# First visit's scores as plain float32 products of two heads on 64 rows each; the value products of a visit as one row

## The chip, the cores and the metric

The kernel runs on one core of one Trainium2 chip. The metric is the device time of one execution in microseconds; the time of a kernel is the median of several runs. A profile comes from one further execution with the hardware profiler on.

The core has five engines that matter here, each working through its own list of instructions in order: TensorE (PE, with its weight loads PEld), VectorE (DVE), ScalarE (ACT), GpSimd (POOL) and SyncE (SP), which issues the DMA transfers.

## The reference, cut to what matters

```
B, H, S, D = 4, 8, 768, 64
q_bucket = bits of (q @ proj > 0), 6 of them, as one number;  k_bucket likewise
scores = q @ k.T / 8, and -1e9 where q_bucket != k_bucket
attn = softmax(scores);  y = attn @ v              # for each batch and head
x = y as [B*S, 512]
out = (relu(x @ w_in) ** 2) @ w_out                # w_in 512 x 2048, w_out 2048 x 512
```

The feed-forward part is called `moe` in the code. The inputs q, k and v are float32; the weights come as 64-bit numbers, of which the kernel makes two float16 parts.

## The kernel before, in words

**Two layers of program.** The body of the kernel does not issue instructions. Each call, as `pe.matmul(...)` or `dve.tensor_scalar(...)`, appends an operation (`Op`) to a `Program`, with its possible engines, its dependencies and a rank. `Program.add` finds the dependencies by comparing the regions that operations touch (`Program.region`); a tile in PSUM counts as one region. `Program.order` then plans: it runs a list scheduler forwards with costs written down in the code (`Program.cost`), computes priorities backwards from the result, and repeats that four times (`ROUNDS`), keeping the shortest plan. `Program.emit` issues everything in that fixed order. So each change of the operations gives a new order of the whole kernel. A call of `matmuls` with several products is one operation, and nothing is placed inside it. Where the planner sees TensorE idle early in the program, `emit` fills part of the gap with products of ones (tile `idle`).

**Units, visits and stages.** A unit is 128 queries of one head against all 768 keys. A visit is a pair of heads and a half of the queries (384): six units. There are 192 units in 32 visits. Batch 0 takes the first halves of its four pairs of heads (visits 0 to 3) and then the second halves (visits 4 to 7); the later batches take both halves of a pair in turn. When the four visits of a batch and a half are there, a stage of the feed-forward part can run on these 384 rows: 16 steps over the hidden dimension, each of 12 products into `pm` (384 columns) and 9 into `po` (512 columns). There are eight stages. `PACE` keeps a product of the stages from running ahead of a given unit. Counted as `pace()` counts, a stage has 112 steps of three products each.

**Preparing a pair of heads** (`prep`). Keys and queries of a head arrive in one tile R, keys on partitions 0 to 63 and queries on 64 to 127. A is their float16 part, L the float16 rest. The signs of the projections (`pd`, `bits`) times a table of signs (`sgn`) give mask codes `pc`, which become M. Five copies by DMA between partitions then build, for each head, stacks of 128 rows: (Q, A) and (M, L). The scores of a unit are four float16 products (two stacks by two halves of the keys) accumulated in `pS`: main parts, cross terms and mask in 128 rows. The A, L, Q and M of four pairs are kept (8 buffers each), so that batch 0 prepares each pair once for both its halves.

**A unit** (`unit`). VectorE takes the scores from PSUM to `e` with the row's extreme, ScalarE takes the exponential with the row's sum, `rv` is its reciprocal. In the first four visits (`PLAIN_AV`) GpSimd multiplies `e` by `rv`, TensorE transposes it into `pT`, and ScalarE or VectorE copies it to `aT` as float32. Later visits make two float16 parts (`hl`) and transpose them by DMA into `aT`. `pS` has one buffer of two banks; until unit 24 every other unit uses the banks of `po`.

**The value products of a visit** (`av`). For both heads, on columns 0 to 63 and 64 to 127 of TensorE, `aT` is multiplied with the values into one bank, `pA`: 6 pairs of float32 products in the first four visits, 18 pairs of float16 products (hi by hi, lo by hi, hi by lo) after them. Each pair is one operation of the planner. The result, as two float16 parts, is `xx`.

**The start.** On SyncE's queue stand the first pair's R, two loads of `proj` to `pj`, eight of the sign table to `sgn_f`, then stacks, weights (`raw`) and further pairs as the planner orders them. Every operation is issued by lines 422 and 425, so the profile's groups are told apart by their tiles.

Of the kernel before, what the change touches and what calls it, by code (L numbers as in the profile page):

```python
# [11 lines left out]
F16 = mybir.dt.float16  # L12
BF16 = mybir.dt.bfloat16
F32 = mybir.dt.float32
# [3 lines left out]
AF = mybir.ActivationFunctionType  # L18
ALU = mybir.AluOpType
# [4 lines left out]
P = 128  # L24
B, H, S, D = 4, 8, 768, 64
NB = 6
HS = 384
UNITS = B * H * S // P
KC = S // P
# [3 lines left out]
BIG = float(2.0**100)  # L33
# [14 lines left out]
PREP, STACKS, VALUES = -9, 0, 2  # L48
# [3 lines left out]
ALTERNATE = {True: 24, False: 0}  # L52

PLAIN_AV, DIVIDE = (0, 1, 2, 3), ("pool",)
# [6 lines left out]
PACE = ((19, 0), (64, 140), (193, 660))  # L61

TOP_BY, LOW_BY = ("dve", "act"), ("dve", "pool")
CHECK_RANK, EARLY = 200, 24


# [61 lines left out]
class Program:  # L128
# [24 lines left out]
    @staticmethod  # L153
    def region(view):
        ap, rec = view.ap, view.rec
        size = lambda dims: 1 + sum(st * (n - 1) for st, n in dims)
        if rec.kind == "dram":
            return 0, 1, ap.offset, ap.offset + size(ap.ap), 0, 0, 0
        p0, f0 = divmod(ap.offset, rec.row)
        if rec.kind == "psum":  # L160
            return 0, 1, 0, 1, 0, 0, 0

        (step, n), inner = ap.ap[1], size(ap.ap[2:])
        block = (step, f0 % step, f0 % step + inner) if n > 1 and f0 % step + inner <= step else (0, 0, 0)
        return (p0, p0 + ap.ap[0][1], f0, f0 + size(ap.ap[1:])) + block
# [281 lines left out]
def run(ctx: ExitStack, tc, kq, v, proj2, w_in, w_out, consts, out, flag):  # L447
    fast = flag is not None
# [5 lines left out]
    pr = Program(tc)  # L454
    pe, dve, act, pool, sp = pr.pe, pr.dve, pr.act, pr.pool, pr.sp
    T, U = slice(0, D), slice(D, P)
# [3 lines left out]
    def send(out, x):  # L460
        sp.dma_start(out, x)
# [15 lines left out]
    def sb(shape, dtype, name, bufs=1, tag=None):  # L477
        return pr.tile(sbp, "sb", shape, dtype, name, bufs_of.get(tag or name, bufs), tag)

    def ps(shape, dtype, name, bufs=1, tag=None):  # L480
        return pr.tile(psp, "psum", shape, dtype, name, bufs, tag)
# [8 lines left out]
        sp.dma_start(cst, consts[:, 0:4])  # L490
    pj = sb([P, 32], F32, "pj")
    dve.memset(pj, 0.0)
    sp.dma_start(pj[:, 0:NB], proj2[:, NB : 2 * NB])
    sp.dma_start(pj[:, NB : 2 * NB], proj2[:, 3 * NB : 4 * NB])
    sgn_f = sb([P, 4 * P], F32, "sgn_f", tag="f" if fast else "o")
    dve.memset(sgn_f, 0.0)
    for n in range(4):
        for t in range(2):
            c0 = 4 + t * D
            sp.dma_start(sgn_f[32 * n + t * NB : 32 * n + (t + 1) * NB, n * P + t * D : n * P + (t + 1) * D], consts[2 * t * NB : (2 * t + 1) * NB, c0 : c0 + D])  # L500
    sgn = sb([P, 4 * P], BF16, "sgn")
    masks = cst
    if fast:
        parts = lambda x: x.rearrange("p (n t d) -> p n t d", t=2, d=D)
        dve.tensor_scalar(parts(sgn)[:, :, 0], parts(sgn_f)[:, :, 0], 2.0 / BIG, 2.0**15, ALU.mult, ALU.mult)
        dve.tensor_scalar(parts(sgn)[:, :, 1], parts(sgn_f)[:, :, 1], 2.0, 2.0**14, ALU.mult, ALU.mult)
        masks = sb([P, 2], F32, "masks")
        dve.memset(masks[T, 0:1], 3 * 2.0**16)
        dve.memset(masks[T, 1:2], -65504.0)
        dve.memset(masks[U, 0:1], 2.0**16)  # L510
        dve.memset(masks[U, 1:2], 0.0)
        balance = 1.0
        maxes, sums = sb([P, UNITS], F32, "maxes"), sb([P, UNITS], F32, "sums")
    else:
        dve.tensor_copy(sgn, sgn_f)
        balance = cst[:, 2:3]
    thr = sb([P, 1], F32, "thr")
    dve.memset(thr, -(2.0**-80))
    unit_f = sb([P, P], F32, "unit_f")
    sp.dma_start(unit_f, consts[:, 4 + 2 * P :])  # L520
    if not fast:
        ident = sb([P, P], BF16, "ident")
        dve.tensor_copy(ident, unit_f)
    ones = sb([P, P], BF16, "ones")
    dve.memset(ones, 1.0)
    pr.idle = ps([P, 512], F32, "idle", tag="pm")[:, 0:P], ones

# [89 lines left out]
    def matmuls(*args, start=True, stop=True):  # L619
        pr.add((pe, "matmuls", [(a, {"start": start, "stop": stop}) for a in args], {}))  # L620

    def prep(b, hp):
# [29 lines left out]
            out.append(((Q, A), (M, L)))  # L652
        return out

    vscales, loaded = {}, {}

    def scale_values(b):
# [36 lines left out]
        return VV  # L694


    def unit(st, half, i, aT, plain):
        c0 = half * HS + i * P
        u = pr.rank
        pS = ps([P, 3, 512], F32, "pS2", tag="po") if u % 2 and u < ALTERNATE[fast] else ps([P, 2, 512], F32, "pS")  # L700
        pr.marks[u] = len(pr.ops)
        pr.rank = u - 1000
        for s, (a, bb) in enumerate(st):
            for j in range(2):
                pe.matmul(pS[:, j, 0:HS], a[:, c0 : c0 + P], bb[:, j * HS : (j + 1) * HS], start=s == 0, stop=s == len(st) - 1)
        sS = pS[:, 0:2, 0:HS]
        e = sb([P, S], F32, "e", bufs_of["e"])
        e2 = e.rearrange("p (j s) -> p j s", j=2)
        if fast:
            nmx, sm = maxes[:, u : u + 1], sums[:, u : u + 1]  # L710
            dve.tensor_scalar(e2, sS, -SC, 2.0**40, ALU.mult, ALU.min, accum_out=nmx)
            act.activation(e2, e2, AF.Exp, bias=nmx, scale=-1.0, accum_out=sm)
        else:
            nmx, sm = sb([P, 1], F32, "nmx", 2), sb([P, 1], F32, "sm", 2)
            dve.tensor_reduce(nmx, sS, AX.XY, ALU.max, negate=True)
            act.activation(e2, sS, AF.Exp, bias=nmx, accum_out=sm)
        pr.rank = u
        rv = sb([P, 1], F32, "rv", 3)
        pr.add(*[(q, "tensor_scalar", (rv, sm, 1e-9, 1.0 if plain else 1.0 / ASC, ALU.add, ALU.mult), {}) for q in (dve, pool)])
        dve.reciprocal(rv, rv)  # L720
        if plain:
            move(e, e, rv, tuple(getattr(pr, k) for k in DIVIDE))
            for g in range(2):
                pT = ps([P, 512], F32, "pT", tag=("pm", "pA")[g] if u < EARLY else "misc")[:, 0:HS]
                pr.busy_from = min(pr.busy_from, len(pr.ops))
                for c in range(3):
                    kc = 3 * g + c
                    pe.matmul(pT[:, c * P : (c + 1) * P], e[:, kc * P : (kc + 1) * P], unit_f, start=True, stop=True, is_transpose=True)
                move(aT[:, 3 * g : 3 * g + 3, i * P : (i + 1) * P], pT.rearrange("p (c s) -> p c s", c=3), 1.0, (act, dve))
            return  # L730
        hl = sb([P, 2, S], F16, "hl", bufs_of["hl"])
        move(hl[:, 0], e, rv)
        left(hl[:, 1], e, rv, hl[:, 0])
        sp.dma_start_transpose(aT[:, :, i * P : (i + 1) * P], hl.rearrange("p t s -> p (t s)"))
# [5 lines left out]
    def av(b, hp, half, VV, aTs):  # L740
        pA = ps([P, 512], F32, "pA")[:, 0:HS]
        plain = VV.dtype == F32
        todo = [(kc, t * D, kc + l * KC) for t, l in (((0, 0),) if plain else ((0, 0), (1, 0), (0, 1))) for kc in range(KC)]
        scale = vscales[b][0] if plain else 1.0 / ASC
        for n, (kc, d0, c) in enumerate(todo):
            matmuls(*[(pA[m], VV[:, h, kc, d0 : d0 + D], aTs[h][:, c]) for h, m in enumerate((T, U))], start=n == 0, stop=n == len(todo) - 1)
        xx = xxs[b, half, hp] = sb([P, 2, HS], F16, "xx")
        move(xx[:, 0], pA, scale)
        left(xx[:, 1], pA, scale, xx[:, 0])
# [151 lines left out]
    kept, kept_v = {}, {}  # L901
    alive = lambda views: all(x.rec in x.rec.line[-x.rec.bufs :] for x in views)

    def ready(b, hp, rank):

        if (b, hp) not in kept or not alive(x for st in kept[b, hp] for ab in st for x in ab):
            pr.rank = rank
            kept[b, hp] = prep(b, hp)

    ready(*visits[0][:2], -10.0)  # L910

    early = {n: (split_win, j, win_rank(4 * j)) for j, n in enumerate(WIN_AT)}
    early[WOUT_AT] = split_wout, 0, conv_rank(0)
    done, u, stages = {}, 0, 0
    for n, (b, hp, half) in enumerate(visits):
        sts, aTs, plain = kept[b, hp], [], fast and n in PLAIN_AV
        for h, st in enumerate(sts):
            aT = sb([P, KC, HS], F32, "aT") if plain else sb([P, 2 * KC, HS], F16, "aT")
            aTs.append(aT)
            for i in range(3):  # L920
                pr.rank = u
                unit(st, half, i, aT, plain)
                u += 1
        if n + 1 < len(visits):
            ready(*visits[n + 1][:2], u + PREP)
        if (b, hp, plain) not in kept_v or not alive([kept_v[b, hp, plain]]):
            pr.rank = u - 6 + PREP
            kept_v[b, hp, plain] = values(b, hp, plain)
        pr.rank = u - 0.5
        av(b, hp, half, kept_v[b, hp, plain], aTs)  # L930
        if n in early:
            do, j, pr.rank = early[n]
            do(j)
        done[b, half] = done.get((b, half), 0) + 1
        if done[b, half] == H // 2:
            moe(stages, b, half)
            stages += 1
# [37 lines left out]
```

## Time and profile before

| | |
|---|---|
| median of 3 runs | 852.07 us (851.78 to 855.12) |
| profiled execution, its own time | 855.38 us |
| its span | 853.6 us |
| PE busy | 816.5 us, 96% |
| ACT busy | 655.9 us, 77% |
| DVE busy | 607.8 us, 71% |
| DMA queue q1, share of 16 engines | 76.6% |
| mean granted clock of TensorE | 0.994 |

An engine's busy time is the union of its instructions' times. A group of instructions is written as engine, operation, output<-input by the names of the tiles, partitions x elements, and count; then the busy time in us and the mean duration in ns of one, and the idle time of the engine just before them with what ended it. TensorE's products are pipelined: a product shows about 0.17 us longer than the time after which the next one starts, so starts are compared, not durations. A float32 product is listed as two instructions.

### The profile page before, as it was taken

How to read it: one execution, taken by the hardware profiler on the slowest of the kernel's cores; microseconds unless marked ns; L12 is line 12 of the kernel's file. 1: busy time of each engine (PE TensorE's matmuls, PEld its weight loads, DVE VectorE, ACT ScalarE, POOL GpSimd, SP SyncE). 2: the span in 40 equal slices, each digit the busy share in tenths (PEclk: the TensorE clock that was granted, in tenths of full speed). 3: DMA queues.
4: the chain of work that ended last, by engine and by line, in shares of the span. 5: the costliest groups of instructions: out<-in, count | busy, mean ns of one | idle time of the engine just before them, and what ended most of it. 6: DMA issues, size and time to landing. Idle time of an engine off the chain costs nothing.

```text
span 853.6 us, 14638 instructions
## 1 busy us (share of the span) xinstructions
PE 816.5 (96%) x5154; PEld 431.1 (51%) x5154; DVE 607.8 (71%) x1218; ACT 655.9 (77%) x1237; POOL 74.7 (9%) x149
## 2 busy tenths in 40 slices
PE   6788799999999999999999999999999999999996
PEld 5544445555555555555555555555554445544553
DVE  5789889998989898998988328999994171163111
ACT  3689999998988898888888557898894298743343
POOL 0246311000001000010100000110000000000000
PEclk9999999999999999999999999999999999999999
DMA  7996689999999999999999229999850089881001
GB/s 211 256 290 192 203 220 191 196 195 190 190 201 178 176 215 179 213 192 194 182 203 220 53 74 193 203 183 185 150 107 1 16 212 282 267 292 61 1 1 41
DMA packets 299297, 145.30 MB, mean 170 GB/s; under 512 B 268880, under 2 KB 279248, under 8 KB 299216
## 3 DMA queue, kind: packets, MB, share of 16 engines
q1 hardware_dynamic: 299216, 144.30, 76.6%
q8 instruction: 42, 0.69, 0.3%
q14 instruction: 39, 0.32, 0.1%
HBM read 56.17 MB, written 6.29 MB: 73 GB/s over the span
## 4 chain that ended last, share of the span: by engine, by line
PE 83%; ACT 6%; DMA 6%; DVE 3%; issue 1%; SPq 0%; POOL 0%; ACTq 0%
PE po L425 28%; PE pm L425 27%; PE pS L425 13%; PE pA L422 11%; DMA raw<-w_out 1%; PE pd L422 1%; ACT e L425 1%; ACT top L425 1%; ACT aT L425 1%; DMA raw<-w_in 1%; DMA X<-vp 1%; DMA V<-vp 1%; PE pc L425 1%; DMA M<-Q 1%; DMA X<-kq 1%
## 5 line engine op out<-in xcount | busy, mean ns | idle before, releaser
L425 PE MATMUL po<-wo,g 128*128 128x512 f16 x1152 | 326.3, 380 | 4.3 <-DVE g L425 3.2
L425 PE MATMUL pm<-xx,win 128*128 128x384 f16 x1536 | 316.0, 326 | 0.9 <-DVE xx L425 0.7
L425 PEld LDWEIGHTS <-win 128*128 128x128 f16 x1536 | 149.5, 98 | 112.5 <-issue 5.2
L425 ACT ACTIVATE e<-e,maxes 128x768 f32<-128x768 f32 x192 | 178.7, 932 | 25.2 <-DVE e L425 22.3
L425 DVE TENSOR_SCALAR_CACHE_REDUCE e<-pS 128x768 f32<-128x768 f32 x192 | 182.7, 953 | 16.4 <-PE pS L425 12.3
L425 DVE SCALAR_TENSOR_TENSOR hl<-e,rv,hl 128x768 f16<-128x768 f32 x168 | 170.8, 1019 | 15.1 <-ACT hl L425 14.3
L425 PEld LDWEIGHTS <-g 128*128 128x128 f16 x1152 | 110.9, 98 | 128.4 <-issue 10.0
L425 DVE SCALAR_TENSOR_TENSOR g<-g,g 128x384 f16<-128x384 f32 x124 | 68.5, 553 | 136.0 <-ACT g L425 132.1
L425 ACT ACTIVATE hl<-e,rv 128x768 f16<-128x768 f32 x168 | 155.0, 924 | 8.3 <-DMA aT<-hl 6.3
L425 ACT ACTIVATE g<-pm 128x384 f32<-128x384 f32 x127 | 61.4, 483 | 110.6 <-PE pm L425 109.5
L425 ACT ACTIVATE g<-g 128x384 f16<-128x384 f32 (+1 forms) x249 | 128.6, 517 | 5.3 <-PE po L425 1.6
L422 PE MATMUL pA<-aT,VV 128*64 128x384 f16 x1008 | 100.0, 331 | 0.0
L425 PE MATMUL pS<-A,Q 128*128 128x384 f16 x384 | 96.4, 330 | 3.3 <-DVE e L425 1.9
L425 PE MATMUL pS<-L,M 128*128 128x384 f16 x384 | 96.1, 328 | 2.0 <-DMA M<-Q 2.0
L425 POOL TENSOR_SCALAR rv<-sums 128x1 f32<-128x1 f32 x113 | 39.1, 346 | 569.0 <-ACT e L425 454.2
L422 PEld LDWEIGHTS <-VV 128*64 128x64 f16 x1008 | 51.8, 109 | 47.3 <-issue 29.8
L425 PEld LDWEIGHTS <-Q 128*128 128x128 f16 x384 | 34.3, 98 | 42.8 <-issue 17.9
L425 PEld LDWEIGHTS <-M 128*128 128x128 f16 x384 | 37.0, 98 | 29.3 <-DMA M<-Q 3.8
L425 DVE TENSOR_SCALAR M<-pc,masks 128x384 f16<-128x384 f32 x64 | 43.0, 671 | 6.6 <-PE pc L425 6.5
L425 ACT ACTIVATION_READ_ACCUMULATOR e<-e,maxes 128x1 f32 x192 | 37.0, 193 | 0.0
L425 DVE SCALAR_TENSOR_TENSOR L<-R,A 128x768 f16<-128x768 f32 x32 | 30.2, 950 | 6.3 <-ACT A L425 6.2
L425 ACT ACTIVATE A<-R 128x768 f16<-128x768 f32 x32 | 26.7, 836 | 8.3 <-DMA R<-kq 8.2
(68 smaller groups left out, 528.7 us busy)
## 6 DMA issues: line engine op xcount, KB each, us to landing
R<-kq SPq DMA_DIRECT2D x32, 384.0 KB
X<-kq SPq DMA_DIRECT2D x32, 384.0 KB
raw<-w_in SPq DMA_DIRECT2D x16, 511.8 KB
raw<-w_out SPq DMA_DIRECT2D x16, 511.8 KB
V<-vp SPq DMA_DIRECT2D x20, 384.0 KB
out<-o SPq DMA_DIRECT2D x24, 256.0 KB
X<-vp SPq DMA_DIRECT2D x16, 384.0 KB
Q<-L SPq DMA_DIRECT2D x32, 96.0 KB
```

Of the source, the lines that this page charges most:

```text
L422: ins = q.engine.matmul(*map(real, args), **kw).ins
L425: ins = getattr(q.engine, o.name)(*map(real, o.args), **{k: real(x) for k, x in o.kw.items()}).ins
```

## The change

It has three parts. The first visit (`WIDE` = 1) is not prepared by `prep`: a new function `first` loads keys K (64 rows of each of the two heads, one head on partitions 0 to 63, the other on 64 to 127) and queries G likewise, and makes mask codes MK and MG of 64 rows with one product for each half of the keys and one for the queries. `side_by_side` then computes the scores as a float32 product of G and K and a float16 product of MG and MK for each half of the keys, the two heads on rows 0 to 63 and 64 to 127; for the first two units the heads are taken one after the other, for the rest a product of each head forms one operation. The units of the two heads then alternate. The pair of heads of visit 0 is prepared by `prep` for visit 4. Second, `av` collects all products of a visit and adds them in operations of up to `2 * RUN` = 36. Third, `Program.region` tells banks of PSUM apart, and the constants come in fewer DMA transfers, with `ones` made earlier.

```
+RUN = 18
+CONSTS_BY, WIDE = ("sp", "sp", "sp"), 1
...
         if rec.kind == "psum":
-            return 0, 1, 0, 1, 0, 0, 0
+            return 0, 1, f0 // 512, 1 + (f0 % rec.row + size(ap.ap[1:]) - 1) // 512, 0, 0, 0
...
-    sp.dma_start(pj[:, 0:NB], proj2[:, NB : 2 * NB])
-    sp.dma_start(pj[:, NB : 2 * NB], proj2[:, 3 * NB : 4 * NB])
+    by[0].dma_start(pj[:, 0 : 3 * NB], proj2[:, NB : 4 * NB])
...
     for n in range(4):
-        for t in range(2):
-            c0 = 4 + t * D
-            sp.dma_start(sgn_f[32 * n + t * NB : 32 * n + (t + 1) * NB, n * P + t * D : n * P + (t + 1) * D], consts[2 * t * NB : (2 * t + 1) * NB, c0 : c0 + D])
+        by[1].dma_start(sgn_f[32 * n : 32 * n + 4 * NB, n * P : (n + 1) * P], consts[0 : 4 * NB, 4 : 4 + P])
...
+        codes = sb([P, 4 * P], BF16, "codes")
+        for t, x in enumerate((2.0 / BIG, 2.0)):
+            for j in range(2):
+                w = slice(2 * j, 2 * j + 2)
+                move(parts(codes)[:, w, t], parts(sgn_f)[:, w, t], x * 2.0 ** (15 - j), (dve,))
...
+    def first(hp):
+
+        K, G = [sb([P, n], F32, name, tag="VV") for name, n in (("K", S), ("G", HS))]
+        for x, w in ((K, T), (G, U)):
+            for odd, m in enumerate((T, U)):
+                send(x[m], kq[0, 2 * hp + odd, w, 0 : x.shape[1]])
+        MK, MG = sb([P, S], F16, "MK", tag="M"), sb([P, HS], F16, "MG", tag="Q")
+        halves = K[:, 0:HS], K[:, HS:], G
+        pd = ps([P, 512], F32, "pd", tag="misc")[:, 0:HS]
+        matmuls(*[(pd[32 * n : 32 * n + 32], pj, x) for n, x in enumerate(halves)])
+        bits = sb([P, HS], BF16, "bits")
+        act.activation(bits[0:96], pd[0:96], AF.Sign, scale=2.0**60, bias=thr[0:96])
+        pc = ps([P, 3, 512], F32, "pc", tag="po")[:, :, 0:HS]
+        for n in range(3):
+            pe.matmul(pc[:, n], codes[0:96, n * P : (n + 1) * P], bits[0:96], start=True, stop=True)
+        for n in range(2):
+            dve.tensor_scalar(MK[:, n * HS : (n + 1) * HS], pc[:, n], 3 * 2.0**16, -65504.0, ALU.subtract, ALU.max)
+        pr.add((act, "activation", (MG, pc[:, 2], AF.Relu), {"bias": shift}), (dve, "tensor_scalar", (MG, pc[:, 2], 2.0**16, 0.0, ALU.subtract, ALU.max), {}))
+        return K, G, MK, MG
+
+    def side_by_side(st, half, i):
+
+        K, G, MK, MG = st
+        c0 = half * HS + i * P
+        pr.rank = u - 1000
+        both = [ps([P, 2, 512], F32, "pS"), ps([P, 3, 512], F32, "pS2", tag="po")]
+        jobs = [[(n, x[:, j, 0:HS], a[m, c0 : c0 + P], bb[m, j * HS : (j + 1) * HS]) for x, m in zip(both, (T, U))] for n, (a, bb) in enumerate(((G, K), (MG, MK))) for j in range(2)]
+        if not i:
+            jobs = [[x[t]] for t in range(2) for x in jobs]
+        for x in jobs:
+            matmuls(*[y[1:] for y in x], start=x[0][0] == 0, stop=x[0][0] == 1)
+        return both
...
+        jobs = []
         for n, (kc, d0, c) in enumerate(todo):
-            matmuls(*[(pA[m], VV[:, h, kc, d0 : d0 + D], aTs[h][:, c]) for h, m in enumerate((T, U))], start=n == 0, stop=n == len(todo) - 1)
+            jobs += [((pA[m], VV[:, h, kc, d0 : d0 + D], aTs[h][:, c]), {"start": n == 0, "stop": n == len(todo) - 1}) for h, m in enumerate((T, U))]
+        for n in range(0, len(jobs), 2 * RUN):
+            pr.add((pe, "matmuls", jobs[n : n + 2 * RUN], {}))
...
+        if fast and visit < WIDE:
+            pr.rank = rank
+            wide[visit] = first(hp)
+        elif (b, hp) not in kept or not alive(x for st in kept[b, hp] for ab in st for x in ab):
             pr.rank = rank
             kept[b, hp] = prep(b, hp)
...
+        if n in wide:
             for i in range(3):
-                pr.rank = u
-                unit(st, half, i, aT, plain)
-                u += 1
+                for aT, pS in zip(aTs, side_by_side(wide[n], half, i)):
+                    pr.rank = u
+                    unit(None, half, i, aT, plain, pS)
+                    u += 1
```

More of the change, by code (lines that the diff above doesn't have):

```diff
@@ L492, in run @@
     dve.memset(pj, 0.0)
-    sp.dma_start(pj[:, 0:NB], proj2[:, NB : 2 * NB])
-    sp.dma_start(pj[:, NB : 2 * NB], proj2[:, 3 * NB : 4 * NB])
+    ones = sb([P, P], BF16, "ones")
+    dve.memset(ones, 1.0)
+    pr.idle = ps([P, 512], F32, "idle", tag="pm")[:, 0:P], ones
+    by = [getattr(pr, x) for x in CONSTS_BY]
+    by[0].dma_start(pj[:, 0 : 3 * NB], proj2[:, NB : 4 * NB])
     sgn_f = sb([P, 4 * P], F32, "sgn_f", tag="f" if fast else "o")
@@ L506, in run @@
         dve.tensor_scalar(parts(sgn)[:, :, 1], parts(sgn_f)[:, :, 1], 2.0, 2.0**14, ALU.mult, ALU.mult)
-        masks = sb([P, 2], F32, "masks")
+        masks = sb([P, 4], F32, "masks")
         dve.memset(masks[T, 0:1], 3 * 2.0**16)
@@ L511, in run @@
         dve.memset(masks[U, 1:2], 0.0)
+        codes = sb([P, 4 * P], BF16, "codes")
[3 more added lines that the diff above has]
+                move(parts(codes)[:, w, t], parts(sgn_f)[:, w, t], x * 2.0 ** (15 - j), (dve,))
+        shift, thr = masks[:, 2:3], masks[:, 3:4]
+        dve.memset(shift, -(2.0**16))
+        dve.memset(thr, -(2.0**-80))
         balance = 1.0
@@ L516, in run @@
         balance = cst[:, 2:3]
-    thr = sb([P, 1], F32, "thr")
-    dve.memset(thr, -(2.0**-80))
+    if not fast:
+        thr = sb([P, 1], F32, "thr")
+        dve.memset(thr, -(2.0**-80))
     unit_f = sb([P, P], F32, "unit_f")
-    sp.dma_start(unit_f, consts[:, 4 + 2 * P :])
+    by[2].dma_start(unit_f, consts[:, 4 + 2 * P :])
     if not fast:
@@ L523, in run @@
         dve.tensor_copy(ident, unit_f)
-    ones = sb([P, P], BF16, "ones")
-    dve.memset(ones, 1.0)
-    pr.idle = ps([P, 512], F32, "idle", tag="pm")[:, 0:P], ones
     win = sb([P, 2, NCC, DFF], F16, "win")
@@ L694, in values, with unit @@
         return VV
-    def unit(st, half, i, aT, plain):
+    def unit(st, half, i, aT, plain, pS=None):
         c0 = half * HS + i * P
         u = pr.rank
-        pS = ps([P, 3, 512], F32, "pS2", tag="po") if u % 2 and u < ALTERNATE[fast] else ps([P, 2, 512], F32, "pS")
         pr.marks[u] = len(pr.ops)
         pr.rank = u - 1000
-        for s, (a, bb) in enumerate(st):
-            for j in range(2):
-                pe.matmul(pS[:, j, 0:HS], a[:, c0 : c0 + P], bb[:, j * HS : (j + 1) * HS], start=s == 0, stop=s == len(st) - 1)
+        if pS is None:
+            pS = ps([P, 3, 512], F32, "pS2", tag="po") if u % 2 and u < ALTERNATE[fast] else ps([P, 2, 512], F32, "pS")
+            for s, (a, bb) in enumerate(st):
+                for j in range(2):
+                    pe.matmul(pS[:, j, 0:HS], a[:, c0 : c0 + P], bb[:, j * HS : (j + 1) * HS], start=s == 0, stop=s == len(st) - 1)
         sS = pS[:, 0:2, 0:HS]
@@ L902, in run, with ready @@
     alive = lambda views: all(x.rec in x.rec.line[-x.rec.bufs :] for x in views)
-    def ready(b, hp, rank):
-        if (b, hp) not in kept or not alive(x for st in kept[b, hp] for ab in st for x in ab):
+    wide = {}
+    def ready(visit, rank):
+        b, hp, _ = visits[visit]
+        if fast and visit < WIDE:
+            pr.rank = rank
+            wide[visit] = first(hp)
+        elif (b, hp) not in kept or not alive(x for st in kept[b, hp] for ab in st for x in ab):
             pr.rank = rank
             kept[b, hp] = prep(b, hp)
-    ready(*visits[0][:2], -10.0)
+    ready(0, -10.0)
     early = {n: (split_win, j, win_rank(4 * j)) for j, n in enumerate(WIN_AT)}
@@ L915, in run @@
     for n, (b, hp, half) in enumerate(visits):
[L916 to L919, printed above, removed]
+        plain = fast and n in PLAIN_AV
+        aTs = [sb([P, KC, HS], F32, "aT") if plain else sb([P, 2 * KC, HS], F16, "aT") for _ in range(2)]
+        if n in wide:
             for i in range(3):
-                pr.rank = u
-                unit(st, half, i, aT, plain)
-                u += 1
+                for aT, pS in zip(aTs, side_by_side(wide[n], half, i)):
+                    pr.rank = u
+                    unit(None, half, i, aT, plain, pS)
+                    u += 1
+        else:
+            for aT, st in zip(aTs, kept[b, hp]):
+                for i in range(3):
+                    pr.rank = u
+                    unit(st, half, i, aT, plain)
+                    u += 1
         if n + 1 < len(visits):
-            ready(*visits[n + 1][:2], u + PREP)
+            ready(n + 1, u + PREP)
         if (b, hp, plain) not in kept_v or not alive([kept_v[b, hp, plain]]):
```

## The prediction

> **What bounds the kernel now.** I read the page's first lines and its chain of waits first, then a table of windows cut where the character of the work changes, and last the order of time on single engines at the two places that the change touches.
>
> ```profile
> span 853.6 us, 14638 instructions
> PE 83%; ACT 6%; DMA 6%; DVE 3%; issue 1%; SPq 0%; POOL 0%; ACTq 0%
> ```
>
> The chain that ends last is TensorE for 83% of the span. Where the other 17% lie, the windows show (columns: stretch, length, busy time of PE, PEld, DVE, ACT, POOL, granted clock, DMA share, GB/s):
>
> ```profile
> 10.00:35.00 25.00, 17.64 (x195) 12.52 (x191) 16.75 (x26) 11.54 (x17) 0.00 (x0) 0.93 0.96 272
> 35.00:60.00 25.00, 20.51 (x130) 11.80 (x131) 20.66 (x46) 22.71 (x48) 14.33 (x19) 0.93 1.00 282
> 60.00:108.00 48.00, 39.13 (x246) 21.76 (x245) 43.11 (x91) 47.45 (x102) 22.37 (x31) 1.00 0.69 209
> 150.00:300.00 150.00, 149.97 (x991) 79.59 (x992) 136.53 (x290) 134.74 (x247) 9.62 (x27) 1.00 1.00 190
> 300.00:475.00 175.00, 175.00 (x1144) 91.84 (x1142) 155.71 (x322) 155.14 (x282) 12.48 (x34) 1.00 1.01 198
> 475.00:700.00 225.00, 224.85 (x1367) 115.88 (x1366) 152.03 (x291) 161.23 (x299) 9.82 (x26) 1.00 0.62 121
> 700.00:841.00 141.00, 137.32 (x755) 69.13 (x753) 39.02 (x68) 77.57 (x169) 0.00 (x0) 1.00 0.47 146
> ```
>
> From 150 us to 841 TensorE is never free for more than 4 us in all: there, time goes away only if TensorE work, or dead time inside its row, goes away. Before 108 us it is another program: ScalarE is busy 47.45 of 48 us from 60 on, VectorE 43.11, and between 10 and 35 us ScalarE stands idle for 25 - 11.54 = 13.5 us while DMA is at 0.96. The handover is the first product of the feed-forward layers (tile pm):
>
> ```profile
> 31.87 0.95 DVE L425 TENSOR_SCALAR_CACHE_REDUCE e<-pS 128x768 f32<-128x768 f32 x1
> 35.21 0.91 ACT L425 ACTIVATE e<-e,maxes 128x768 f32<-128x768 f32 x1
> ...
> 109.50 1.95 PE L425 MATMUL pm<-xx,win 128*128 128x384 f16 x11 [0.68 <-DVE xx L425]
> ```
>
> So the first unit's scores reach VectorE at 31.87 us, its exponential starts at 35.21, and layers of the first half can run from 109.5 on, released by the last xx of visit 3. Everything earlier than that is paid as TensorE's time without its filler.
>
> **The values' products in one row.** The row of one pair of value products among products of the layers, and the one visit that already runs in one piece, stand so in order of time:
>
> ```profile
> 774.60 0.35 PE L422 MATMUL pA<-aT,VV 128*64 128x384 f16 x2
> 774.89 0.39 PE L425 MATMUL po<-wo,g 128*128 128x512 f16 x1
> 775.21 0.35 PE L422 MATMUL pA<-aT,VV 128*64 128x384 f16 x2
> ...
> 506.19 3.12 PE L422 MATMUL pA<-aT,VV 128*64 128x384 f16 x36
> 509.24 2.12 PE L425 MATMUL po<-wo,g 128*128 128x512 f16 x9
> ```
>
> Nine po in a row last 2.12 us with the last one's 0.39, so one follows another after (2.12 - 0.39)/8 = 0.216 us. The 36 of a whole visit, 18 pairs that run two at a time, take 509.24 - 506.19 = 3.05 us with their exit, so a pair is at most 0.169 and, with an exit of some 0.12, 0.163 us. The alternating stretch repeats after 775.21 - 774.60 = 0.61 us: 0.61 - 0.163 - 0.216 = 0.23 us of each turn is neither product. It is the price of going from the 128*128 shape to 128*64 and back, and the rows call it busy. There are 95 such rows of f16 value products, the first and the last of them being
>
> ```profile
> 143.60 0.52 PE L422 MATMUL pA<-aT,VV 128*64 128x384 f16 x4
> 780.05 0.35 PE L422 MATMUL pA<-aT,VV 128*64 128x384 f16 x2
> ```
>
> for 28 visits. After the change each visit's 36 products are one operation of the planner (twice RUN), so 28 rows are left: 67 turns less, 67 x 0.23 = 15.4 us of TensorE's row. Their place decides what they are worth: 11 of the 67 lie before 300 us, 14 from 300 to 475, 42 after. After 475 nothing but TensorE is near its limit (VectorE 152 of 225 us, DMA 0.62), and those 42, 9.7 us, come off the end. Before 475 the units (scores, exponential, transposes) run beside DMA at 1.00 and VectorE at 0.91 of the time, and TensorE can only use what it saves if it has layers' products waiting. Up to 300 us it has done
>
> ```profile
> L425 PE MATMUL pm<-xx,win 128*128 128x384 f16 x352 | 66.2, 326 | 0.9 <-DVE xx L425 0.7 <-ACT g L425 0.2
> L425 PE MATMUL po<-wo,g 128*128 128x512 f16 x252 | 64.5, 380 | 0.7 <-ACT g L425 0.4 <-DVE g L425 0.2
> L425 PE MATMUL pS<-A,Q 128*128 128x384 f16 x178 | 45.3, 333 | 3.1 <-DVE e L425 1.7 <-DMA A<-A 1.3
> ```
>
> (352 + 252)/3 = 201 of the 224 steps that the first two of eight stages hold, at unit 178/2 = 89, and the third stage needs visit 14, which ends with unit 90 and some time for its transposes. 23 steps are 23 x 3 x (0.163 + 0.216)/2 = 13 us of stock, just enough. So the 11 x 0.23 = 2.5 us saved before 300 may only bring a wait forward: bounds 0 and 2.5, and I take half, as the units themselves are freed a little. This part gives 15.4 - 1.3 = 14.1 us, bounds 9.7 and 15.4.
>
> The edit has a cost: a score product that comes up during a visit's block waits up to 3.05 us, and behind it VectorE's e, ScalarE's exponential and the transposes of that unit. What hides it is that VectorE and ScalarE have other work (splits of earlier units, squares of the layers) and that no unit is on the chain after 475. If that cover is gone it costs what the stock of 13 us can't hold.
>
> The Trainium skill, TensorEngine Tiling (Array Packing), section Tiling Modes, says that a change of tiling mode drains TensorE; the 0.23 us agree, and by that rule the scores on 64 rows below pay it too, whose shape no row shows. At the 0.23 us of the rows, twelve operations of the first visit would pay 2.8 us, before 35 us, where it is covered as their own time is.
>
> **The first visit.** Removed from the start: two splits (A, L), ten copies that build the stacks, four mask products with their four M, and the wait for them. Added: K and G loaded to 64 rows for each of two heads, three mask products, float32 score products. Removed, the work comes back: the keys and queries of the same pair of heads are prepared for visit 4, between 60 and 108 us.
>
> When are the first scores there? Their inputs' chain is the one that can be read from the old start up to its first mask:
>
> ```profile
> 7.15 0.85 PE L422 MATMUL pd<-R,pj 128*32 128x384 f32 x8
> 9.77 0.68 DVE L425 TENSOR_SCALAR M<-pc,masks 128x384 f16<-128x384 f32 x1 [2.36 <-PE pc L425]
> ...
> 86.29 4.09 PE L422 MATMUL pA<-aT,V 128*64 128x384 f32 x24 [1.22 <-ACT aT L425]
> 90.31 0.34 PE L425 MATMUL pS<-A,Q 128*128 128x384 f16 x1
> ```
>
> The masks are ready at about 9.77 + 3 x 0.68 = 11.8 us, ahead of any stack. No row shows a float32 product on 64 rows. The nearest are the float32 value products, which run in pairs on 64 columns: (90.31 - 86.29)/6 = 0.67 us a pair. If rows pair as columns do, the visit costs 4 x 0.67 + 4 x 0.163 for its first two units, done singly, and as much for the other four: 6.7 us; if they don't pair, 10.0; the old 24 products cost 24 x 0.163 = 3.9. I take 6.7, the row of the same width. The difference, 2.8 to 6.1 us, lies between 10 and 35 us, where 25 - 17.64 = 7.4 us of TensorE are free, beside the products that the program puts in only to keep it busy. It costs the end nothing, at most it puts the sixth unit 6 us later, long before 35.
>
> The clock in those windows is 0.93, not 1.00. The Trainium skill, TensorE: Matmul & The Clock Gate, Part 1, says that the clock is either full or half and falls to half after an idle window of about 3.4 us. By that page alone a cold first visit would take 13.4 us in place of 6.7, and the units would still be through before 35.
>
> So six units start at about 13 us in place of 31.87. On ScalarE a unit is
>
> ```profile
> L425 ACT ACTIVATE e<-e,maxes 128x768 f32<-128x768 f32 x27 | 25.6, 953 | 0.0
> L425 ACT ACTIVATE aT<-pT 128x384 f32<-128x384 f32 x46 | 21.6, 505 | 2.8 <-PE pT L425 2.7
> L425 ACT ACTIVATE A<-R 128x768 f16<-128x768 f32 x9 | 7.7, 850 | 7.2 <-DMA R<-kq 7.0
> L425 DVE TENSOR_SCALAR_CACHE_REDUCE e<-pS 128x768 f32<-128x768 f32 x27 | 25.3, 951 | 1.6 <-PE pT L425 1.6
> L425 DVE TENSOR_SCALAR M<-pc,masks 128x384 f16<-128x384 f32 x17 | 11.4, 672 | 4.7 <-PE pc L425 4.7
> L425 DVE SCALAR_TENSOR_TENSOR L<-R,A 128x768 f16<-128x768 f32 x8 | 7.6, 956 | 4.3 <-ACT A L425 4.3
> ```
>
> 25.6/27 = 0.95 us of exponential and 2 x 21.6/46 = 0.94 of copies, 1.9 us, six times 11.3 us. All of it now lies after 35 us and would fit the 13.5 us that ScalarE idles before. Of the work that comes back, two A are 1.7 us: ScalarE's load from 35 to 108 falls from 70.2 to 60.6 of 73 us. VectorE is the next one late. It loses four of the six e (two were already before 35), 3.8 us, and gets two L and four M, 1.9 + 2.7 = 4.6, so its 20.66 + 43.11 = 63.8 stay 64.6 us. Were it never idle, the stretch would last 64.6 in place of 73, 8.4 us less; at the 96% that ScalarE holds there now (70.2 of 73) it lasts 67.3, 5.7 us less. DMA gets two R of 384 KB and ten stacks of 96 KB, 1.7 MB, at 209 GB/s 8 us; from 60 to 108 us it has 0.31 x 48 = 15 us free. I take 5.7, bounds 0 (visit 1's stacks come no sooner) and 8.4.
>
> The rest has one answer. Fewer, larger loads of constants, the ones and memsets moved ahead, codes from sgn_f (four small VectorE operations of some 0.3 us) lie before 10 us, under the loads. Regions of PSUM by bank free the planner's order among banks and remove no instruction. K and G sit in two of the five value buffers and are given back before the fourth value is needed.
>
> **Sum.** The profiled execution took 855.38 us, 1.8 more than its span, and 3.3 more than the median of 852.07. 855.38 - 14.1 - 5.7 = 835.6; the same 19.8 off the median are 832.3. With both at their bounds: 852.07 - 23.8 = 828.3 to 852.07 - 9.7 = 842.4.
>
> **Rivals.**
> - Only the value products pay. Visit 1 still waits for its stacks, which queue behind weights on a DMA at 1.00 from 35 to 60 us, so the engines are early with visit 0 and idle after it. For it: that share, and that the weights' conversions, which would fill the gap, wait for DMA too. Against it: ten stacks fewer are in that queue. 852.07 - 14.1 = 838.
> - Only the start pays. The units run at the pace of DMA and VectorE, TensorE's stock of layers' products runs dry, and what the rows save turns into waits, also late. For it: the stock of 13 us at 300. Against it: 42 of 67 turns lie after 475. 852.07 - 5.7 = 846.4.
> - Slower: a block stands in TensorE's row ahead of work that is ready, and waits at its head for the last transposed probabilities, because the fixed order was made with transposes that land sooner than they do with DMA at 1.00. The float32 block above already waited 1.22 us for its input. At this price in each of 28 visits it is 34 us, and 852.07 + 34 - 19.8 = 866; it outweighs the gains from 19.8/28 = 0.71 us a visit on. Against it: no f16 row of value products had any idle time ahead of it.
> - It doesn't do what it says in time: the whole order is planned anew, and a worse order later (an early pause of the units, a late weight) eats the 20 us. 852.
>
> **How the numbers follow.** The forecast has 0.60, the value products alone 0.20, the start alone 0.06, the wait at the block 0.06, no change 0.08. A measurement of this kernel can tell 0.5%, 4.3 us, from no change: faster is 0.60 + 0.20 + 0.06 = 0.86, same 0.08, slower 0.06. The predicted time is 832.3. The range goes from 824, 4 us under the bound for what a new order may add, to 847, which takes in the first two rivals; some 0.16 are left out.
>
> **What would show it.** Right: 28 rows of f16 value products of 36, each about 3.05 us to the next start, no idle time ahead of them; first e on VectorE at 12 to 14 us, the first pm at about 103 and TensorE full from there; VectorE at 95% or more before it. Wrong: the first pm at 109 as now with ScalarE idle between 30 and 45 us (the first rival); TensorE idle around 300 us with pm waiting for xx (the second); value products with a wait on DMA of the transposes ahead of them (the third). Float32 rows of the first visit whose starts are 0.67 us apart for each head, not for two, would show that rows don't pair.

## The result and the profile after

| | before | after |
|---|---|---|
| median of four runs each, in one comparison | 852.86 us | 833.34 us (830.51 to 834.86) |
| ratio, 95% interval | | 0.9764 (0.973 to 0.9798) |
| profiled execution | 855.38 us | 834.86 us |
| its span | 853.6 us | 833.1 us |

The forecast was 832.3 us. The page's head, after:

```profile
span 833.1 us, 14383 instructions
PE 794.3 (95%) x5001; PEld 430.0 (52%) x5001; DVE 605.2 (73%) x1200; ACT 656.6 (79%) x1238; POOL 72.7 (9%) x175
```

TensorE's busy time fell by 816.5 - 794.3 = 22.2 us, the others' hardly. To see where, I cut both traces at the handover, the first pm. First the windows of before, then those of after (columns as in the prediction):

```profile
0.00:108.50 108.50, 84.79 (x652) 52.59 (x653) 85.44 (x177) 85.75 (x170) 37.20 (x55) 0.97 0.80 231
108.50:853.60 745.10, 731.66 (x4504) 378.54 (x4502) 522.37 (x1042) 570.15 (x1068) 37.47 (x95) 1.00 0.77 161
```

```profile
0.00:97.70 97.70, 74.65 (x485) 43.33 (x485) 79.60 (x175) 80.62 (x162) 36.09 (x53) 0.97 0.83 242
97.70:833.10 735.40, 719.65 (x4517) 386.65 (x4516) 525.58 (x1026) 575.96 (x1077) 36.65 (x122) 1.00 0.77 166
```

The handover comes 108.5 - 97.7 = 10.8 us sooner, and what follows it is 745.1 - 735.4 = 9.7 us shorter. Behind the handover TensorE is busy 12.0 us less and idle 735.4 - 719.65 = 15.8 us, 2.3 more than the 13.4 before.

The order of time at the start, after: VectorE's first e, TensorE's first pm, and the xx of visits 0 and 3.

```profile
13.79 0.95 DVE L427 TENSOR_SCALAR_CACHE_REDUCE e<-pS 128x768 f32<-128x768 f32 x1
43.21 0.55 DVE L427 SCALAR_TENSOR_TENSOR xx<-pA,xx 128x384 f16<-128x384 f32 x1
...
98.00 0.55 DVE L427 SCALAR_TENSOR_TENSOR xx<-pA,xx 128x384 f16<-128x384 f32 x1
```

```profile
97.70 0.32 PE L427 MATMUL pm<-xx,win 128*128 128x384 f16 x1 [1.04 <-ACT xx L427]
```

In the trace of before, the xx of visits 0 and 3 start at

```profile
59.06 0.54 DVE L425 SCALAR_TENSOR_TENSOR xx<-pA,xx 128x384 f16<-128x384 f32 x1
...
108.89 0.56 DVE L425 SCALAR_TENSOR_TENSOR xx<-pA,xx 128x384 f16<-128x384 f32 x1
```

The first unit starts 18 us sooner, visit 0 ends 15.9 us sooner, visit 3 only 10.9: a visit takes (98.00 - 43.21)/3 = 18.3 us where it took 16.6. A third of the head start is given back on the way.

The float32 scores on 64 rows, first of one head alone, then of both together, and behind the latter the float16 part and the next row:

```profile
6.78 1.55 PE L424 MATMUL pS<-K,G 64*128 64x384 f32 x4
8.27 0.52 PE L424 MATMUL pd<-K,pj 128*32 128x384 f32 x2
...
22.14 1.56 PE L424 MATMUL pS<-K,G 64*128 64x384 f32 x8
23.53 0.49 PE L424 MATMUL pS<-MK,MG 64*128 64x384 f16 x4
23.95 0.85 PE L424 MATMUL pd<-R,pj 128*32 128x384 f32 x8
```

A float32 product is listed as two, so x4 is two products and x8 four. Four take 23.53 - 22.14 = 1.39 us, two alone 1.49 with the change of shape behind them: two heads on 64 rows each run at once, 0.70 us a pair.

The value products of the last visit that has them, after:

```profile
708.54 1.67 PE L427 MATMUL po<-wo,g 128*128 128x512 f16 x7
710.15 3.12 PE L424 MATMUL pA<-aT,VV 128*64 128x384 f16 x36
713.20 1.80 PE L427 MATMUL pm<-xx,win 128*128 128x384 f16 x10
```

All 28 visits stand so, 36 in 3.05 us. The group of the f16 value products over the whole page:

```profile
L424 PE MATMUL pA<-aT,VV 128*64 128x384 f16 x1008 | 87.2, 327 | 0.0
```

The same group before:

```profile
L422 PE MATMUL pA<-aT,VV 128*64 128x384 f16 x1008 | 100.0, 331 | 0.0
```

No idle time ahead of them, as before; 12.8 us of their busy time are gone. What was hardly there before is a wait at the end of the stages. TensorE's waits behind the handover, the longest three, after:

```profile
PE po L427 <- ACT o L427: 5.7, 8, 0.9
PE pm L427 <- ACT g L427: 2.8, 5, 1.0
PE pm L427 <- ACT xx L427: 1.5, 2, 1.0
```

The same wait of po before:

```profile
PE po L425 <- ACT o L425: 0.2, 1, 0.2
```

One of the eight, on ScalarE and on TensorE:

```profile
200.23 0.60 ACT L427 ACTIVATE o<-po 128x512 f32<-128x512 f32 x1 [0.16 <-PE po L427]
```

```profile
199.38 0.81 PE L427 MATMUL po<-wo,g 128*128 128x512 f16 x3
200.88 0.59 PE L427 MATMUL po<-wo,g 128*128 128x512 f16 x2 [0.69 <-ACT o L427]
```

The planner, which now tells banks apart, puts the copy of one finished bank ahead of the products into the next; the issued program makes the product wait for the copy of the same tile.

### The profile page after: what moved, and what is told of

Same layout as the page of the kernel before. It is cut to its first block, busy times and chain, and to the rows that moved or that the text cites. A ratio compares the mean times of both kernels' runs of the same rounds, so it can differ in the third digit from the quotient of the medians.

```text
span 833.1 us, 14383 instructions
## 1 busy us (share of the span) xinstructions
PE 794.3 (95%) x5001; PEld 430.0 (52%) x5001; DVE 605.2 (73%) x1200; ACT 656.6 (79%) x1238; POOL 72.7 (9%) x175
## 5 line engine op out<-in xcount | busy, mean ns | idle before, releaser
L427 PE MATMUL po<-wo,g 128*128 128x512 f16 x1152 | 296.9, 379 | 5.7 <-ACT o L427 5.7
L427 PE MATMUL pm<-xx,win 128*128 128x384 f16 x1536 | 297.7, 326 | 4.4 <-ACT g L427 2.8
L427 ACT ACTIVATE e<-e,maxes 128x768 f32<-128x768 f32 x192 | 178.2, 929 | 20.7 <-DVE e L427 19.2
L427 ACT ACTIVATE g<-g 128x384 f32<-128x384 f32 (+1 forms) x251 | 129.4, 517 | 6.6 <-PE po L427 2.7
L427 PE MATMUL pS<-A,Q 128*128 128x384 f16 x372 | 93.1, 330 | 4.1 <-DVE e L427 2.6
L427 PE MATMUL pS<-L,M 128*128 128x384 f16 x372 | 91.8, 327 | 0.8 <-DMA M<-Q 0.8
L424 PE MATMUL pA<-aT,VV 128*64 128x384 f16 x1008 | 87.2, 327 | 0.0
L427 POOL TENSOR_SCALAR rv<-sums 128x1 f32<-128x1 f32 x136 | 36.8, 271 | 541.7 <-ACT e L427 400.2
L424 PEld LDWEIGHTS <-VV 128*64 128x64 f16 x1008 | 54.7, 110 | 32.9 <-issue 10.0
L427 PEld LDWEIGHTS <-Q 128*128 128x128 f16 x372 | 34.2, 98 | 43.1 <-issue 16.2
L427 DVE TENSOR_SCALAR M<-pc,masks 128x384 f16<-128x384 f32 x64 | 43.0, 672 | 15.4 <-PE pc L427 15.2
L427 PE MATMUL pT<-unit_f,e 128*128 128x128 f32 x144 | 23.8, 293 | 10.5 <-ACT aT L427 7.7
```

Source lines behind the costliest of these rows:

```text
L424: ins = q.engine.matmul(*map(real, args), **kw).ins
L427: ins = getattr(q.engine, o.name)(*map(real, o.args), **{k: real(x) for k, x in o.kw.items()}).ins
```

## The experiments

The theory going in: the handover is worth what it moves (10.8 us), each row of value products less is worth 0.22 us (entry 0.09, exit 0.12, the medians over the rows' starts), and the regions by bank cost the 5.7 us of waits, which is why 10.8 and 14.7 don't make 25.5 but 20.5. The rival: the gains behind the handover are limited by the pace of the units. All times are medians of five to twelve runs, beside runs of the kernel before on the same chip (852.7 to 853.3 us).

**One row a visit, alone.** The kernel before with `av` of the change and RUN = 18:

```
-            matmuls(*[... for h, m in enumerate((T, U))], start=..., stop=...)
+        for n in range(0, len(jobs), 2 * RUN):
+            pr.add((pe, "matmuls", jobs[n : n + 2 * RUN], {}))
```

> The kernel before with one edit: a visit's value products as one operation. Theory (each row of value products costs TensorE 0.22 us beside its products, and 67 rows fewer come off the end): 28 rows of 36, first pm at 109 us as before, TensorE's busy time less by 14 us, time 852.9 - 14 = 839. Rival (the units' pace up to 475 us can't use what is saved there, so 25 of the 67 turns become waits of pm or po): 852.9 - 9 = 844, with new idle time of TensorE between 150 and 475 us.

Measured: 839.48 us, ratio 0.9853 (0.9828 to 0.9879), 13.2 us less. Its windows:

```profile
0.00:107.70 107.70, 85.16 (x645) 51.95 (x646) 87.58 (x179) 85.63 (x168) 39.37 (x55) 0.97 0.80 230
107.70:835.50 727.80, 715.44 (x4498) 386.05 (x4502) 519.03 (x1019) 568.40 (x1068) 47.25 (x118) 1.00 0.78 166
```

28 rows, the handover 0.8 us sooner, TensorE idle behind it 12.4 us (13.4 before). The turns are worth their price and nothing turned into waits: the rival falls for this part.

**All but the one row.** The changed kernel with each pair an operation again:

```
-RUN = 18
+RUN = 1
```

> The changed kernel with RUN = 1: each pair of value products is an operation of its own again, all else as changed. Theory (start worth 11 us by the first pm at 97.7 in place of 108.5 us, regions by bank cost 5.7 us in waits of po for o): about 95 rows of value products again, 833.3 + 14 = 847. Rival (the start's gain is given back later, and all that was gained is the rows'): 852 or more.

Measured: 839.09 us, ratio 0.9847 (0.9826 to 0.9867). Neither expectation holds: the pairs again cost only 5.8 us. The trace has 52 rows of f16 value products, not 95, and the handover at 97.5. 24 rows more than 28, x 0.22 = 5.3 us, fit the price; what was wrong is the number of rows. Something else in the change already joins them.

**Regions by bank, alone.** The kernel before with

```
-            return 0, 1, 0, 1, 0, 0, 0
+            return 0, 1, f0 // 512, 1 + (f0 % rec.row + size(ap.ap[1:]) - 1) // 512, 0, 0, 0
```

> The kernel before with one edit: regions of PSUM by bank. Theory: waits of po for ACT o of 0.7 us each appear, some 5 us in all, 852.9 + 5 = 858. Rival (the freer order among banks gains as much as the waits cost, or the waits come only with the other parts of the change): 853, within 1.5.

Measured: 845.31 us, ratio 0.9909 (0.989 to 0.9928): 7.4 us less where the theory said 5 more. The waits of po for ACT o are there, 3.4 us in 5, but there are 59 rows in place of 95, and rows of a single pair fall from 34 to 5. 36 x 0.22 = 7.9 us. Its windows:

```profile
0.00:106.20 106.20, 83.56 (x639) 50.87 (x640) 83.33 (x176) 84.13 (x166) 38.62 (x52) 0.97 0.79 234
106.20:843.90 737.70, 724.14 (x4506) 382.44 (x4507) 523.19 (x1048) 572.99 (x1072) 32.37 (x91) 1.00 0.77 163
```

TensorE's idle time behind the handover is 13.6 us, as before (13.4): the waits took the place of others. By the code, nine po of a step were one chain for the planner and are three now; that this is why it no longer alternates them with pairs, as it did between 774 and 780 us, is read from the order and not tested by itself.

**The change without the regions by bank**, the same line undone in the changed kernel.

> The changed kernel with a PSUM tile as one region again. Theory (the planner, told of banks, places the copy of a stage's first bank ahead of the products into the other two; the program's waits are for the whole tile, so TensorE stands for each such copy, 5.7 us in 8 waits of po for ACT o): those waits fall to the 0.2 us of the kernel before, 833.3 - 5.5 = 828. Rival (the waits stand where TensorE would have idled anyway, or a new order costs as much elsewhere): 833, within 1.5.

Measured: 832.37 us, ratio 0.9756 (0.9734 to 0.9778), the same as the change. The rival was right: po no longer waits for ACT o, and TensorE's idle time behind the handover is 15.8 us as with them. Beside one row a visit the regions are worth nothing.

**Banks, but the copies behind all products.**

```
                         move(o, po[:, t], back)
+                        pr.ops[-1].deps |= {j for j in po.rec.ops if pr.ops[j].ways[0][0] is pe}
```

> The changed kernel with regions by bank, but each copy of a stage's result placed by the planner behind all of the stage's products, as the program's waits have it. Theory (the 5.7 us of waits of po for ACT o are lost time): they fall below 0.5 us and the time is 833 - 5 = 828. Rival (as with whole tiles: the same time is lost in other waits behind the handover, whose idle time of TensorE stayed 15.8 us): 832 to 834.

Measured: 833.56 us, ratio 0.9765 (0.9742 to 0.9788). Its TensorE waits behind the handover:

```profile
PE pm L427 <- ACT g L427: 2.9, 3, 1.1
PE po L427 <- ACT g L427: 1.8, 4, 1.1
PE pS L427 <- DVE e L427: 1.0, 3, 0.4
PE pm L427 <- ACT xx L427: 0.7, 1, 0.7
PE po L427 <- ACT o L427: 0.4, 2, 0.2
```

The eight waits are gone, idle is 15.5 us in place of 15.8, and the time is the same. A second way to the same end: in both orders without these waits, other idle time of TensorE stands in their place.

**All but the first visit.** The changed kernel with its first visit prepared as before:

```
-CONSTS_BY, WIDE = ("sp", "sp", "sp"), 1
+CONSTS_BY, WIDE = ("sp", "sp", "sp"), 0
```

> The changed kernel with WIDE = 0: the first visit is prepared as before, all else as changed. Theory (the handover, the first pm, comes 10.8 us earlier by the first visit's scores alone, the fewer loads of constants are worth nothing): first pm at about 107 us, 28 rows of value products, 833 + 10 = 843. By the sum of the parts run alone it is at least the kernel before with one row a visit, 839.5. Rival (the constants and the earlier ones bring a share of the start): first pm at 103 or sooner and 838 or less.

Measured: 845.98 us, ratio 0.992 (0.9894 to 0.9946), the handover at 109.2 us, 28 rows. So the constants bring nothing that this order shows, and the first visit is worth 846.0 - 833.3 = 12.7 us against it. But the kernel should not be slower than the one with only the rows joined (839.5), and it is by 6.5: behind the handover TensorE is idle 733.4 - 717.28 = 16.1 us in place of 12.4, and the handover is 1.5 us later. That raised the question how much an order alone is worth.

**The fifth pair late.** The kernel before; the preparing for visit 8 held until unit 24.

```
-            pr.rank = rank
+            pr.rank, pr.mark = rank, 24 if (b, hp) == (1, 0) else None
             kept[b, hp] = prep(b, hp)
+            pr.mark = None
```

> The kernel before, with the preparing of the fifth pair of heads (for visit 8) held until unit 24, that is behind visit 3. Theory (VectorE and ScalarE set the handover by the work they do before it, and the change won more there than forecast because its buffers put the fifth pair behind the handover): first pm about 3 to 4 us sooner, 105, and time 852.7 - 3 = 849.5. Rival (visit 0's late start sets the handover, and what else is done before it doesn't matter): first pm 108.5 and 852.7.

Measured: 852.99 us, ratio 1.0012 (0.9991 to 1.0034), the handover at 106.9. Half of the expected 3 to 4 us, and none of it in the time. But the hold moved little. Eight of the L belong to the first four pairs; a ninth, of the fifth pair, stands ahead of the handover in the kernel before, and one still does with the hold, since unit 24 starts before visit 3 is through. Before, then with the hold:

```profile
108.03 0.94 DVE L425 SCALAR_TENSOR_TENSOR L<-R,A 128x768 f16<-128x768 f32 x1
```

```profile
105.34 0.96 DVE L425 SCALAR_TENSOR_TENSOR L<-R,A 128x768 f16<-128x768 f32 x1
```

Ahead of the handover VectorE is busy 84.5 us in place of 85.4, and ScalarE 84.8 in place of 85.8. So this run does not test whether their load sets the handover.

**Two visits wide**, WIDE = 2, and **visits 4 to 7 in the order of pairs 1, 2, 3, 0**:

```
-... + [(b, hp, 1) for hp in range(F, H // 2)]
+... + [(b, hp, 1) for hp in ((1, 2, 3, 0) if fast and b == 0 else range(F, H // 2))]
```

> The changed kernel with WIDE = 2: visits 0 and 1 both as float32 scores on 64 rows. Theory (handover set by VectorE and ScalarE before it: one more pair's two L and four M, 4.6 us of VectorE, moves behind it): first pm at about 94 us, time 830. Rival (K and G of two visits hold four of five value buffers, and the values of visits 1 and 2 come late; or VectorE's work just moves to visit 5): first pm at 98 or later, time 833 or more.

> The changed kernel with visits 4 to 7 in the order of pairs 1, 2, 3, 0, so that the pair of visit 0, which has no stacks, is prepared for visit 7 and not for visit 4. Theory (the same: 4.6 us of VectorE and 2.3 us of ScalarE leave the time before the handover): first pm at about 94 us, time 829 to 830. Rival (the work that leaves is replaced by weights' conversions that have to be done before the layers anyway): first pm at 97 to 98, 833.

Measured: 844.47 us (0.9906, 0.988 to 0.9933), handover at 109.4; and 840.77 us (0.9851, 0.9821 to 0.988), handover at 101.4. Both are later than the change's 97.7, where the theory said 94. The windows ahead of the handover, of WIDE = 2 and of the other order:

```profile
0.00:109.40 109.40, 89.69 (x506) 46.94 (x507) 83.20 (x181) 87.70 (x175) 46.82 (x61) 0.89 0.81 239
0.00:101.40 101.40, 79.41 (x493) 42.12 (x494) 81.89 (x181) 84.78 (x170) 42.53 (x56) 0.98 0.83 243
```

The work that was to leave did not: eight (one of them on GpSimd) and nine L stand ahead of the handover, where the change has eight, and VectorE and ScalarE are both busy longer than the change's 79.6 and 80.6 us. So neither run shows what less work would do. For WIDE = 2 the rival's 98 us and 833 or later hold; for the other order the rival was right that the work is replaced, but not on the time. The granted clock with WIDE = 2 is 0.89 there, for the change's 0.97; what part of its delay comes from that was not tested.

**Weights late.** The changed kernel; the later blocks of weights held until unit 24:

```
                 j = f // 4 + FIRST
+                pr.mark = 24
...
                 split_wout(f // 4 + 1)
+                pr.mark = None
```

> The changed kernel, with the weights' blocks beyond the first three (ten of the 22 conversions that it does before the handover) held until unit 24. Theory (the handover is set by what ScalarE and VectorE do before it; ten conversions are 14 us of each): first pm at 90 us or sooner, and time 833 - 5 or better, as long as the conversions come before their layers. Rival (visits 1 to 3 are paced by the chain of each unit, scores, exponential, product with rv, transposes, copies, and the conversions only fill gaps): first pm at 95 to 98, and time 833 or more, since the conversions then press on the units behind the handover, where VectorE is busy 0.91 of the time.

Measured: 843.11 us, ratio 0.9864 (0.984 to 0.9888). The hold moves six conversions and not ten: 16 of VectorE's f stand ahead of the handover, for 22. It comes at 94.8 us, 2.9 sooner for 6 us less of VectorE's and 6.7 less of ScalarE's work; and behind it

```profile
PE pS L427 <- DVE e L427: 12.3, 2, 11.2
PE po L427 <- ACT o L427: 6.2, 9, 0.7
PE pm L427 <- ACT g L427: 3.0, 5, 1.0
```

The conversions stand in VectorE's row, the scores wait for e once for 11.2 us, and TensorE has nothing else. The granted clock is 0.50 from 118.0 to 131.7 us, so the first 4.5 us of products behind that wait, from 127.2 on, also run slower. In this order the earlier handover was paid for by work that is missing right behind it. The rival was right on the time and all but right on the handover (95 to 98 us); the theory's 90 did not come.

**Two other orders of the same operations.** The changed kernel with another lag between engines in the planner:

```
-AHEAD, DELAY, LAG = 60, 2500, 1.0
+AHEAD, DELAY, LAG = 60, 2500, 1.05        # and 0.95
```

> The changed kernel with nothing changed in its operations, only the planner's lag between engines 1.05 in place of 1.0, which gives another order. If the start's gain belongs to the operations: first pm at 97 to 102 us, 28 rows, time within 4 of 833. If it was the luck of one order: first pm anywhere from 97 to 109, time up to 845.

> The same with the lag 0.95. As for the run before: 97 to 102 us and 829 to 837 if the gain belongs to the operations, else up to 109 and 845.

Measured: 841.21 us (0.9851, 0.9833 to 0.987 of the kernel before on that chip: 853.3) and 844.95 us (0.9903, 0.9883 to 0.9924). Windows of the first, and of the second:

```profile
0.00:102.40 102.40, 79.63 (x505) 43.50 (x506) 81.82 (x182) 86.45 (x174) 42.03 (x55) 0.97 0.82 243
102.40:840.50 738.10, 717.37 (x4495) 386.50 (x4499) 519.48 (x1017) 570.12 (x1066) 43.01 (x121) 1.00 0.77 164
```

```profile
0.00:100.90 100.90, 77.94 (x502) 43.77 (x503) 81.63 (x182) 85.72 (x171) 37.57 (x54) 0.98 0.84 246
100.90:842.60 741.70, 721.08 (x4507) 386.69 (x4505) 521.35 (x1028) 574.92 (x1075) 29.33 (x105) 0.99 0.76 163
```

28 rows in both, the handover at 102.4 and 100.9 us, within or just past what was expected if the gain belongs to the operations. The time expected with it, within 4 us of 833, was missed: it is 8 and 12 us above the change's. 4.7 and 3.2 us of it are the handover, and TensorE is idle behind it 20.7 and 20.6 us, 5 more. An order alone is worth up to 12 us here.

All fourteen profiles fit one sum to within some 6 us. Behind the handover stand about 707 us of products (1152 po at 0.2155, 1536 pm at 0.162, 1008 pA at 0.082, some 657 pS at 0.163, and 20 us of smaller ones), the rows' turns, and TensorE's idle time. The last column is what the sum leaves unexplained:

| kernel | handover | rows x 0.22 | idle behind | span | span less the sum with 707 |
|---|---|---|---|---|---|
| before | 108.5 | 20.9 | 13.4 | 853.6 | 3.8 |
| one row, alone | 107.7 | 6.2 | 12.4 | 835.5 | 2.2 |
| banks, alone | 106.2 | 13.0 | 13.6 | 843.9 | 4.1 |
| fifth pair late | 106.9 | 21.6 | 11.0 | 851.0 | 4.5 |
| WIDE = 0 | 109.2 | 6.2 | 16.1 | 842.6 | 4.1 |
| the change | 97.7 | 6.2 | 15.8 | 833.1 | 6.4 |
| RUN = 1 | 97.5 | 11.4 | 14.9 | 838.1 | 7.3 |
| whole tiles | 98.0 | 6.2 | 15.8 | 832.5 | 5.5 |
| copies behind all | 98.6 | 6.2 | 15.5 | 831.3 | 4.0 |
| order 1, 2, 3, 0 | 101.4 | 6.2 | 19.5 | 841.4 | 7.3 |
| lag 1.05 | 102.4 | 6.2 | 20.7 | 840.5 | 4.2 |
| lag 0.95 | 100.9 | 6.2 | 20.6 | 842.6 | 7.9 |
| weights late | 94.8 | 6.2 | 28.7 | 843.6 | 6.9 |
| WIDE = 2 | 109.4 | 6.2 | 15.1 | 842.1 | 4.4 |

## Why the prediction was right

**The value products.** The price of a turn (0.23 us forecast) was right: the three comparisons that change little but the rows and the order give 13.2 + 5.8 + 7.4 = 26.4 us for 67 + 24 + 36 = 127 rows, 0.21 us each. Since an order alone can move the time by up to 12 us, the surer evidence is TensorE's busy time behind the handover: 731.66 - 715.44 = 16.2 us less for the 67 rows, 731.66 - 724.14 = 7.5 for the 36. Alone the part gave 13.2 us, for 14.1 forecast. That a wait at a block's head could eat it fell in the trace: no idle time ahead of any. The doubt about the turns before 300 us hardly mattered: TensorE's idle time of the change between 310 and 360 us is 1.2 us, where it was none. The Trainium skill, TensorEngine Tiling (Array Packing), section Tiling Modes, gives the drain at a change of mode without a price; here it is 0.09 us in and 0.12 out.

**The regions by bank** were costed at nothing because they "remove no instruction", and that reason failed: alone they give 7.4 us, with 36 rows less. They and the joined visits take the same turns, so beside the joined visits they add nothing (whole tiles: the same time). The term was right in the sum, but not for the reason given.

**The start** was under-sized: 5.7 us forecast with a bound of 8.4, the handover 10.8 us sooner. Its reckoning failed too. It let VectorE's work between 35 us and the handover stay at 64.6 us and raised VectorE's share of that stretch to 96%. The stretch before, and after:

```profile
35.00:108.50 73.50, 60.15 (x378) 33.85 (x379) 64.27 (x137) 70.66 (x150) 37.00 (x51) 0.98 0.79 233
```

```profile
35.00:97.70 62.70, 50.07 (x315) 28.20 (x315) 55.59 (x118) 58.67 (x122) 28.41 (x38) 0.97 0.78 233
```

VectorE's share is 55.59 of 62.7 us, 89%, where it was 87%: the sign of 95% or more did not come. What fell is its work there, by 8.7 us. Of these, 2.8 now lie before 35 us, and 85.44 - 79.60 = 5.8 behind the handover: fewer conversions and a half pair less are done before it:

```profile
L427 DVE SCALAR_TENSOR_TENSOR f<-raw,top 128x512 uint32<-128x512 uint32 x22 | 15.3, 698 | 0.9 <-ACT top L427 0.9
L427 DVE SCALAR_TENSOR_TENSOR L<-R,A 128x768 f16<-128x768 f32 x8 | 7.6, 950 | 4.1 <-ACT A L427 4.1
```

(25 and 9 before.) One part of the step did come true: ScalarE uses time in which it idled. Ahead of the handover its idle time fell from 108.5 - 85.75 = 22.8 to 97.7 - 80.62 = 17.1 us. In all five kernels without the first visit wide it is 22.1 to 22.8 us, in the seven with that visit alone wide whose weights are not held 15.2 to 17.2. This fall of 5.7 us equals the forecast's 5.7 by chance, since that came from VectorE's share; the other 5.1 us of the handover are ScalarE's work, 85.75 - 80.62. Whether this work sets the handover or only fills the time up to it stays open. The one run that took work away (weights late, 6.7 us of ScalarE's) came 2.9 us sooner, with 3.8 us more of ScalarE's idle time.

**What was given back.** 10.8 us and 67 x 0.22 = 14.7 us make 25.5, and the span fell by 20.5. Behind the handover there are 1.8 us more of products (14 that stood ahead of it before: eight of pd, four of pS, two of pc), 2.3 us more of idle time and 0.9 us unexplained. That the forecast's sum came out so close is luck: the start's shortfall, 5.1 us, met these 5.

**The float32 scores** pair on rows as on columns, at 0.70 us a pair for the 0.67 taken, and they lie where TensorE has room. The clock of 10 to 35 us was 0.93 again; the half clock that the Trainium skill, TensorE: Matmul & The Clock Gate, Part 1, allows for did not fall on these products, since at half clock a pair would have taken 1.4 us.

**What stays open.** Eight kernels with the first visit alone wide hand over at 94.8 to 102.4 us, five without at 106.2 to 109.2, means 98.9 and 107.7: that the handover comes sooner belongs to the operations. (WIDE = 2, which has the second visit wide as well, hands over at 109.4; why is open.) How much of it reaches the end does not: three orders of the change's own operations give 833.3, 841.2 and 845.0 us, and the one order without the first visit 846.0. Other orders of that kernel were not run. So the change as it stands is worth 19.5 us; the 14.7 us of turns are missing from TensorE's row in each of its orders, and what the start adds, or other waits take back, lies with the order: against WIDE = 0 it is between 1 and 13 us. Against the kernel before with one row a visit (839.5 us), which has no wide first visit either, the three orders are 6.2 us faster, 1.7 slower and 5.5 slower. That the start brings the end any time is therefore not shown.

## What to carry to other kernels

Read a product's price from start to start, across a change of shape too: 0.22 us for each row is called busy in every view, and shows only where rows of two shapes alternate. Before adding up parts, ask which of them remove the same thing; and where a planner lays out the whole order, run the same operations in a second and third order before a gain of one per cent is put down to an edit.

## What the runs showed of the hardware

Two heads' float32 products on 64 rows each, in two tiles of PSUM, run at the pace of one: 0.70 us a pair of 384 columns, and 0.16 us for a float16 pair. Going from 64*128 to 128*32 costs 0.09 us: from 23.53 to 23.95 us stand two float16 pairs of 0.163 us and 0.09 us of change, where 128*64 to 128*128 costs 0.12. Taking away 5.7 us of TensorE's waits bought nothing in two different orders, in which its idle time was 15.8 and 15.5 us, as with them.
